# Window attention and a Mish MLP: two chunks at a time by seven half-matrix products, with weight sums streamed from DRAM

## The chip, the core and the metric

The kernel runs on one core of a Trainium2 chip. A core has five engines with an instruction queue each: TensorE (PE) multiplies matrices into PSUM, VectorE (DVE), ScalarE (ACT) and GpSimd (POOL) work on tiles, SyncE (SP) here issues DMAs. The metric is device time in microseconds (us) of one execution; a kernel's time is the median of its runs.

## What is computed

```python
scores = scale * q @ k.T + bias          # 8 batches, 8 heads, 576 tokens, 64 wide; window of 128, causal
attn = exp(scores - max) / (sum + 1e-9)
x = (attn @ v) as [4608 tokens, 512]
h = x @ w_in                              # 512 x 2048
g = h * tanh(log1p(exp(h)))               # Mish
out = g @ w_out                           # 2048 x 512
```

q, k and v are float32, both weights float64 and used with a precision near float32's.

## The kernel before

**Chunks.** The tokens go through the MLP in nine chunks of 512: chunks 0 to 7 are the first 512 tokens of each batch, chunk 8 is the 64 left over from each, which `last_unit` writes to the DRAM tile `xs` and `last_x` reads back. (The change counts them 1 to 9.)

**Split products.** A float32 operand is split into an upper part rounded to TensorE's float32r and a lower part, the rest. A product of two is three matmuls: upper by upper, upper by lower, lower by upper. The upper part is a copy on ACT, the lower one a subtraction on POOL (for attention's output on DVE). Weights are loaded as float64 bits, put together by `convert_w` from shifts on DVE and copies on ACT, split, and stay in SBUF for the whole kernel, sixteen tiles of the tag "w".

**First product** (`first`, line 433): per group of 256 hidden features, 2 x 12 matmuls of 512 tokens, weights stationary, into a double PSUM tile "s"; ACT applies Mish as it reads it, 128x1024 at a time. Eight groups: 192 matmuls.

**Second product** (`parts`, line 452, and `second`, line 484): for half a chunk (256 tokens) and 256 hidden features, `parts` makes gh (ACT) and gl (POOL), 128x512 each, and twelve matmuls use them: the tokens' parts are stationary, 512 columns of w_out move. Sixteen such groups: 192 matmuls. Three buffers each of gh and gl.

**Attention** (`unit` and `last_unit`): per pair of heads two halves; scores (PE), bias and maximum (DVE), exponential (ACT), fold (POOL), scaling (DVE, for the first batch POOL), transposes (PE), masks (DVE), product with v (PE). The attention of chunk c + 1 is put between the matmuls of chunk c's second product.

**Order.** `run` lists of (position, step) are sorted and emitted; PE's and SP's instructions keep that order (`InOrder`, line 20), those of the other engines are placed by the scheduler, with exponentials, Mish and Sign held in order. Loads and stores are issued on SP, in order.

**PSUM.** "s" takes two buffers of two banks, "o" (attention's output), "w" (transposes of `last_unit`), "po0" and "po1" one bank each.

## Time and profile before

| | us |
|---|---|
| runs | 1069.47, 1072.22, 1071.94; median 1071.94 |
| profiled execution, first to last instruction | 1069.5 |
| attention of the first batch, until the first MLP matmul | 88.4 |
| chunk 0 and attention of the second batch | 88.4 to 223.4 |
| a chunk with attention beside it | 111.2 |
| chunks 7 and 8, without attention | 87.0 each |
| DMA traffic | 59.32 MB |

The result lists the times of three runs; for the profiled execution there is the span alone, and it equals the lowest run. The few microseconds outside a span (launch, the last stores) are not in the trace. "Busy" is the time in which an engine's instructions ran; an idle gap is put down to the engine that released the wait. The granted TensorE clock is a share of full speed.

### The profile page before, as it was taken

What the parts mean: (1) busy time and instruction counts of PE and PEld (TensorE: products, weight loads), DVE (VectorE), ACT (ScalarE), POOL (GpSimd) and SP (SyncE); (2) the same over time, 40 slices, a digit from 0 to 9 for tenths busy, and PEclk for the clock granted to TensorE, in tenths of its full rate; (3) what the DMA queues carried; (4) which work ended last, traced back from release to release, by engine and by line L of the source; (5) the groups of instructions that cost most, each with busy time, mean ns of one, the idle gap of its engine ahead of it and who ended that gap; (6) DMA issues with size and microseconds to landing.
All of it is one profiled execution on the core that took longest, in us unless ns stands there. A gap on an engine that the chain in (4) does not pass through costs nothing.

```text
span 1069.5 us, 14242 instructions
## 1 busy us (share of the span) xinstructions
PE 999.0 (93%) x5280; PEld 786.4 (74%) x5280; DVE 418.9 (39%) x1155; ACT 398.6 (37%) x937; POOL 330.8 (31%) x281
## 2 busy tenths in 40 slices
PE   3547985999999999999999999999999999999998
PEld 2336863788778877787778777877788778888886
DVE  4788088710762057304650375027601770000000
ACT  3454455421543245324432353234333442221221
POOL 2464557510441034202421233114310440042032
PEclk9667997999999999999999999999999999999999
DMA  8940011300221002200320021002200201000001
GB/s 277 398 150 4 1 65 36 90 32 1 60 62 62 1 29 88 68 1 25 92 67 1 24 85 56 21 9 72 72 32 1 61 32 42 10 31 20 1 1 40
DMA packets 52133, 59.32 MB, mean 55 GB/s; under 512 B 13024, under 2 KB 32608, under 8 KB 52064
## 3 DMA queue, kind: packets, MB, share of 16 engines
q1 hardware_dynamic: 50880, 57.69, 16.8%
q8 instruction: 42, 0.69, 0.3%
q10 hardware_dynamic: 1184, 0.72, 0.2%
q14 instruction: 27, 0.22, 0.1%
HBM read 47.91 MB, written 10.49 MB: 55 GB/s over the span
## 4 chain that ended last, share of the span: by engine, by line
PE 82%; POOL 1%; ACT 0%; DVE 0%; issue 0%; POOLq 0%
PE po L30 36%; PE h L30 33%; PE s L30 8%; PE o L30 5%; POOL gl L30 0%; POOL so L30 0%; PE pt_3l L30 0%; PE pt_2l L30 0%; PE pt_1l L30 0%; PE pt_0l L30 0%; DVE pz L30 0%; ACT to L30 0%; ACT ob L30 0%; ACT so L30 0%; POOLq L30 0%
## 5 line engine op out<-in xcount | busy, mean ns | idle before, releaser
L30 PE MATMUL h<-x,si 128*128 128x512 f32 x1728 | 394.6, 390 | 0.0
L30 PEld LDWEIGHTS h<-x,si 128*128 128x128 f32 x1728 | 325.2, 188 | 68.0 <-issue 0.3
L30 PE MATMUL po<-so,gh 128*128 128x512 f32 x1152 | 326.5, 405 | 5.0 <-POOL so L30 2.4
L30 POOL TENSOR_TENSOR gl<-g,gh 128x512 fp32r<-128x512 f32 x144 | 195.2, 1356 | 370.6 <-ACT gh L30 346.0
L30 PEld LDWEIGHTS po<-so,gh 128*128 128x128 f32 x1152 | 207.7, 190 | 55.4 <-ACT x L30 6.6
L30 DVE CUSTOM_DVE_ANT_0 pz<-s,nb 128x256 f32<-128x256 f32 (+1 forms) x256 | 84.6, 387 | 339.9 <-PE s L30 339.9
L30 PE MATMUL po<-so,gl 128*128 128x512 f32 x576 | 179.6, 393 | 0.7 <-POOL gl L30 0.7
L30 ACT ACTIVATE g<-h 128x1024 f32<-128x1024 f32 x72 | 74.0, 1028 | 267.7 <-PE h L30 267.7
L30 ACT ACTIVATE pz<-pz,mx 128x256 f32<-128x256 f32 (+1 forms) x256 | 120.3, 471 | 111.8 <-DVE mx L30 111.7
L30 POOL TENSOR_TENSOR pz<-pz 128x256 f32<-128x256 f32 x64 | 65.3, 1020 | 309.6 <-PE po L30 170.0
L30 ACT ACTIVATE gh<-g 128x512 fp32r<-128x512 f32 x144 | 90.6, 629 | 115.2 <-PE po L30 110.8
L30 PEld LDWEIGHTS po<-so,gl 128*128 128x128 f32 x576 | 108.8, 189 | 25.2 <-POOL gl L30 1.1
L30 DVE TENSOR_TENSOR pz<-s,masks 128x1024 f32<-128x1024 f32 x64 | 78.2, 1223 | 28.7 <-PE s L30 28.7
L30 DVE TENSOR_TENSOR pz<-pz,sm 128x512 f32<-128x512 f32 x56 | 59.3, 1058 | 9.4 <-POOL pz L30 7.3
L30 DVE COPY ob<-po 128x512 f32<-128x512 f32 x18 | 12.4, 691 | 124.8 <-PE po L30 124.8
L30 PE MATMUL s<-ident,pz 128*128 128x128 f32 x256 | 41.9, 290 | 19.7 <-DVE pz L30 10.4
L30 PE MATMUL s<-qk 64*128 64x128 f32 (+1 forms) x448 | 57.7, 376 | 0.0
L30 PEld LDWEIGHTS s<-ident,pz 128*128 128x128 f32 x256 | 33.1, 148 | 31.1 <-POOL pz L30 10.5
L30 PE MATMUL o<-pz,va 128*64 128x128 f32 (+1 forms) x560 | 54.9, 325 | 0.0
L30 PEld LDWEIGHTS o<-pz,va 128*64 128x64 f32 x560 | 33.3, 136 | 27.8 <-issue 9.5
L30 ACT ACTIVATE x<-o 128x512 fp32r<-128x512 f32 x32 | 19.1, 598 | 84.1 <-PE o L30 84.1
L30 ACT ACTIVATION_READ_ACCUMULATOR pz<-pz,mx 128x1 f32 x256 | 48.0, 187 | 0.0
(122 smaller groups left out, 577.4 us busy)
## 6 DMA issues: line engine op xcount, KB each, us to landing
wi<-in_moe_w_in_dram SPq DMA_DIRECT2D x16, 512.0 KB, 10.1
wo<-in_moe_w_out_dram SPq DMA_DIRECT2D x16, 512.0 KB, 10.2
out_dram<-ob SPq DMA_DIRECT2D x32, 256.0 KB, 2.0
qk<-in_q_dram SPq DMA_DIRECT2D x28, 288.0 KB, 3.6
qk<-in_k_dram SPq DMA_DIRECT2D x28, 288.0 KB, 3.9
va<-in_v_dram SPq DMA_DIRECT2D x28, 256.0 KB, 2.9
first<-in_q_dram SPq DMA_DIRECT2D x4, 288.0 KB, 4.1
first<-in_k_dram SPq DMA_DIRECT2D x4, 288.0 KB, 4.4
```

What stands on the lines that cost most here:

```text
L30: ins = method(*args, **kwargs)
```

## The change

Chunk 1 is computed as before in plain products, but with weights stationary in both, and output in transposed form. Chunks 2 to 9 go in four pairs. For a pair, the two products are seen as 2x2 blocks: the contraction in halves, the outputs in halves, and the pair's two chunks as the halves of the tokens. Strassen's form in Winograd's variant then takes seven block products instead of eight:

- of the weights, A11, A12, A22 and the sums S1 to S4; of the tokens, B11, B21, B22 and the sums T1 to T4 (`ORDER_I`, `ORDER_O`, `MOVING`);
- first product (`quad`): for each of eight tiles t of the hidden features, seven products of six matmuls with 512 moving columns; p1, s5 and one output are copied by ACT, four sums of PSUM and SBUF are DVE's, one sum of two SBUF tiles is POOL's. Mish (`mish_of`) works afterwards in SBUF on 128x2048, two tiles in a row;
- second product (`right`, `second`): for each of the seven products m and each of eight tiles t, gh and gl of 128x512 and six matmuls; where the block is one of T1 to T4, DVE first adds or subtracts two quarters of the tile g, in place;
- `prepare`: a pair's token blocks come from raw attention output; 8 sums on DVE, 14 splits of 128x512 (ACT and POOL), most of them during the second product of the pair before. For pair 4 the left-over tokens are loaded from `xs` four steps before it begins.

The weights no longer stay in SBUF. `convert_w` also writes each value to DRAM (`vals_i`, `vals_o`, on ACT's DMA queue); `keep_plain` writes the split A11, A12 and A22 there; `combine` reads values back, makes S1 to S4 on POOL, splits them (ACT, POOL on 128x2048) and writes them out: for w_in in the second product of chunk 1, for w_out in the first product of pair 1. `load_stream` brings the split blocks back, 30 loads of 0.75 or 1 MB for each pair, three buffers, each issued when the buffer's last user is past.

PSUM: four single banks for products, "s" one buffer, "t" one bank for the transposes, "o" one. Attention of two batches is spread evenly over chunk 1 (batches 2 and 3) and over pairs 1 and 2; pair 3 carries the last batch, pair 4 none. The output is stored transposed and put in order on the host.

```diff
+ORDER_I = ("A11", "S1", "A12", "S2", "S3", "S4", "A22")
+ORDER_O = ("A11", "S3", "S2", "A22", "S1", "S4", "A12")
+MOVING = {"A11": "B11", "A12": "B21", "A22": "T4", "S1": "T1", "S2": "T2", "S3": "T3", "S4": "B22"}
...
+    def combine(kind, jj, make_hi, make_lo):
...
+        def work():
+            hi, lo = make_hi(f"Sh{kind}{jj}", F32R), make_lo(f"Sl{kind}{jj}", F32R)
+            tt = pool.tensor_tensor
+            tt(out=V[:, 0], in0=V[:, 2], in1=V[:, 0], op=ALU.add)
+            tt(out=V[:, 2], in0=V[:, 1], in1=V[:, 2], op=ALU.subtract)
+            tt(out=V[:, 1], in0=V[:, 0], in1=V[:, 1], op=ALU.subtract)
+            tt(out=V[:, 3], in0=V[:, 3], in1=V[:, 1], op=ALU.subtract)
+            flat = V.rearrange("p b n -> p (b n)")
+            act.activation(hi, flat, AF.Copy)
+            tt(out=lo, in0=flat, in1=hi.bitcast(F32), op=ALU.subtract)
...
+    def split_x(n, blk, pos, src):
...
+        act.activation(x[:, 0, :], src, AF.Copy)
+        pool.tensor_tensor(out=x[:, 1, :], in0=src, in1=x[:, 0, :].bitcast(F32), op=ALU.subtract)
...
+    def halves_of(key, src):
+        gh = small(0, f"gh{key}", F32R)
+        gl = small(1, f"gl{key}", F32R)
         act.activation(gh, src, AF.Copy)
         pool.tensor_tensor(out=gl, in0=src, in1=gh.bitcast(F32), op=ALU.subtract)
+        parts[key] = (gh, gl)
...
+    def quad(n, t, m):
...
+        b = {"A11": 0, "A12": 0, "S1": 1, "S4": 1, "S2": 2, "S3": 3, "A22": 3}[blk]
+        fresh = blk in ("A11", "S1", "S2", "S3")
...
+        for pos in range(2):
+            for w_, x_ in ((0, 0), (0, 1), (1, 0)):
                 k += 1
                 pe.matmul(
+                    o, lhsT=w[:, w_, pos * P : (pos + 1) * P], rhs=x[:, pos, x_, :],
+                    start=(fresh and k == 1), stop=(k == 6), skip_group_check=True,
                 )
...
+            act.activation(qs["p1"], o, AF.Copy)
...
+            dve.tensor_tensor(out=qs["c"], in0=o, in1=qs["s5"], op=ALU.add)
...
+            pool.tensor_tensor(out=g[:, 3, :], in0=qs["c"], in1=qs["u"], op=ALU.add)
+            dve.tensor_tensor(out=g[:, 2, :], in0=o, in1=qs["u"], op=ALU.add)
...
+    def right(n, m, t):
...
+        new = {
+            "T3": (1, 3, 1, ALU.subtract), "T2": (1, 1, 0, ALU.add),
+            "T4": (0, 2, 1, ALU.subtract), "T1": (1, 3, 1, ALU.subtract),
+        }.get(blk)
+        if new:
+            o, a, b, op = new
+            dve.tensor_tensor(out=g[:, o, :], in0=g[:, a, :], in1=g[:, b, :], op=op)
+        at_ = new[0] if new else {"B11": 0, "B12": 1, "B21": 2, "B22": 3}[blk]
+        halves_of(f"{n + 1}_{m}_{t}", g[:, at_, :])
...
+    def second(n, m, t):
...
+            for k, (g, w_) in enumerate(((gh, 0), (gh, 1), (gl, 0))):
+                pe.matmul(
+                    o, lhsT=w[:, w_, d * P : (d + 1) * P], rhs=g,
...
+        for t in range(NT):
+            for m in range(7):
+                steps.append((7 * t + m, lambda t=t, m=m: quad(n, t, m)))
+            steps.append((14 * (t // 2) + 15.2 + 0.01 * (t % 2), lambda t=t: mish_of(n, t)))
+        for m in range(7):
+            for t in range(NT):
+                at_ = 7 * NT + NT * m + t
+                steps.append((at_, lambda m=m, t=t: second(n, m, t)))
+                steps.append((at_ - 2.4, lambda m=m, t=t: right(n, m, t)))
```

More of the change, by code (lines that the diff above doesn't have):

```diff
@@ L196, in load_first @@
         cs = slice(p * P, (p + 1) * P)
-        t = big(f"first{p}", F32)
+        t = (stream if p < 3 else big)(f"first{p}", F32)
         qk = t[:, : 2 * S].rearrange("p (a s) -> p a s", a=2)
@@ L235, in attention_mish_mlp, with raw_x @@
     HEAD = [slice(i * D, (i + 1) * D) for i in range(2)]
+    def raw_x(n, h):
+        if (n, h) not in xr:
+            xr[n, h] = xp.tile([P, 2, 2, CH], F32, tag=f"x{h}", name=f"xr{n}_{h}")
+        return xr[n, h]
     def unit(b, p, half):
@@ new lines, in second_plain @@
+    def second_plain(i):
+        j, a = divmod(i, 2)
+        gh, gl = parts.pop(f"0_{i}")
+        for d in range(4):
+            if i == 0:
+                po[d] = bank(d, f"p0_{d}")
+            for n, (g, w_) in enumerate(((gh, 0), (gh, 1), (gl, 0))):
+                col = 1024 * a + 512 * w_ + P * d
+                pe.matmul(
+                    po[d], lhsT=split[("o", j)][:, col : col + P], rhs=g,
+                    start=(i == 0 and n == 0), stop=(i == NF - 1 and n == 2),
+                )
+            if i == NF - 1:
+                if d == 0:
+                    obs[0] = stage("ob0").rearrange("p (d n) -> p d n", n=CH)
+                ob = obs[0][:, d, :]
+                if d % 2:
+                    act.activation(ob, po[d], AF.Copy)
+                else:
+                    dve.tensor_copy(ob, po[d])
@@ new lines, in store_out @@
+    def store_out(n, d, r, c):
+        load(out[d, :, 2 * n + 1 + c, :], obs[n + 1, d % 2][:, r, :])
+    def second(n, m, t):
+        blk = ORDER_O[m]
+        gh, gl = parts.pop(f"{n + 1}_{m}_{t}")
+        w = wst[n, 2 * NT + 2 * m + t // 4][:, t % 4]
+        upper = blk in ("A11", "S2", "S1", "S4")
+        fresh = blk in ("A11", "S3", "S2", "S1", "A12")
+        for d in range(2):
+            b = 2 * (not upper) + d
+            if t == 0 and fresh:
+                po[b] = bank((0, 2, 1, 3)[b], f"p{n + 1}_{m}_{d}")
+            o = po[b]
+            for k, (g, w_) in enumerate(((gh, 0), (gh, 1), (gl, 0))):
+                pe.matmul(
+                    o, lhsT=w[:, w_, d * P : (d + 1) * P], rhs=g,
+                    start=(fresh and t == 0 and k == 0), stop=(t == NT - 1 and k == 2),
+                    skip_group_check=True,
+                )
+            if t < NT - 1:
+                continue
+            if m == 0:
+                obs[n + 1, d] = stage(f"ob{n + 1}_{d}").rearrange("p (r n) -> p r n", n=CH)
+            p1, u, c, y = (obs[n + 1, d][:, r, :] for r in range(4))
+            add = dve.tensor_tensor
+            if blk == "A11":
+                act.activation(p1, o, AF.Copy)
+            elif blk == "S3":
+                act.activation(c, o, AF.Copy)
+            elif blk == "S2":
+                add(out=u, in0=o, in1=p1, op=ALU.add)
+                pool.tensor_tensor(out=c, in0=c, in1=u, op=ALU.add)
+            elif blk == "A22":
+                add(out=y, in0=o, in1=u, op=ALU.add)
+            elif blk == "S1":
+                add(out=c, in0=o, in1=c, op=ALU.add)
+            elif blk == "S4":
+                add(out=u, in0=o, in1=u, op=ALU.add)
+            elif blk == "A12":
+                add(out=p1, in0=o, in1=p1, op=ALU.add)
@@ L507, in attention_mish_mlp, with run @@
+    DONE = {"A22": (2, 3, 0), "S1": (2, 2, 1), "S4": (0, 1, 1), "A12": (0, 0, 0)}
+    def run(steps):
+        for _, work in sorted(steps, key=lambda s: s[0]):
+            work()
     for p in range(NP):
         load_first(0, p)
-    conv = [(kind, j) for kind in "io" for j in range(NJ)]
-    for w in conv[:-1]:
-        load_w(*w)
+    for j in range(NJ):
+        load_w("i", j)
+    for j in range(3):
+        load_w("o", j)
+    conv = [("i", j) for j in range(NJ)] + [("o", j) for j in range(NJ)]
@@ new lines, in attention_mish_mlp, with spread, of_first @@
+    steps = attention(0) + [(k, lambda: convert_next(2)) for k in (3.6, 5.6, 7.6)]
+    run(steps)
+    def spread(batches, start, space):
+        return [(start + space * (2 * NP * i + s), f) for i, b in enumerate(batches) for s, f in attention(b)]
+    steps = []
+    for i in range(NF):
+        def of_first(i=i):
+            while ("i", i // 2) not in split:
+                convert_next(0)
+            first_plain(i)
+            if i % 2:
+                convert_next(0)
+        steps.append((2 * i, of_first))
+        if i % 2:
+            steps.append((2 * i + 0.2, lambda j=i // 2: keep_plain("i", j)))
+            if 3 + i // 2 < NJ:
+                steps.append((2 * i + 0.3, lambda j=3 + i // 2: load_w("o", j)))
+        if i % 4 == 3:
+            steps.append((2 * i + 2.5, lambda i=i: mish(g0[i // 4].rearrange("p f n -> p (f n)"))))
@@ new lines, in attention_mish_mlp, with of_second @@
+    for i in range(NF):
+        def of_second(i=i):
+            while ("o", i // 2) not in split:
+                convert_next(1)
+            second_plain(i)
+        steps.append((32 + 2 * i, of_second))
+        steps.append((32 + 2 * i - 4.5, lambda i=i: halves_of(f"0_{i}", g0[i // 4][:, i % 4, :])))
+        if i % 2:
+            steps.append((32 + 2 * i + 0.2, lambda j=i // 2: keep_plain("o", j)))
+            steps.append((32 + 2 * i + 0.3, lambda: convert_next(1)))
+    steps.append((65.5, lambda: load(out[:, :, 0, :].rearrange("d p n -> p d n"), obs[0])))
```

389 lines of the change are left out of this document (253 added, 136 removed).

## The prediction

> **What bounds the kernel now.** First the page's busy times and its span in 40 slices: PE = TensorE, DVE = VectorE, ACT = ScalarE, POOL = GpSimd.
>
> ```profile
> PE 999.0 (93%) x5280; PEld 786.4 (74%) x5280; DVE 418.9 (39%) x1155; ACT 398.6 (37%) x937; POOL 330.8 (31%) x281
> PE   3547985999999999999999999999999999999998
> POOL 2464557510441034202421233114310440042032
> ```
>
> PE is full from the ninth slice (about 215 us) to the end; before that it is not. Then the chain of waits in order of time (start, length, what):
>
> ```profile
> 223.43 43.52 PE h L30 x192
> ...
> 334.67 43.52 PE h L30 x192
> ...
> 890.83 43.52 PE h L30 x192
> 934.35 43.52 PE po L30 x192
> ```
>
> 192 matmuls of 512 columns take 43.52 us, 0.2267 us each, in either MLP product. A chunk with attention takes 334.67 - 223.43 = 111.24 us, and 111.24 - 2 x 43.52 = 24.2 us of that is one batch of attention. Third, busy times by stage:
>
> ```profile
> core 0: us, PE busy (x) PEld busy (x) DVE busy (x) ACT busy (x) POOL busy (x), PEclk, DMA share, GB/s
> 0.00:88.40 88.40, 38.63 (x229) 25.99 (x229) 62.73 (x159) 36.92 (x103) 38.61 (x50) 0.73 0.72 251
> 88.40:134.80 46.40, 46.40 (x207) 37.94 (x205) 17.76 (x26) 25.23 (x37) 24.87 (x19) 0.97 0.02 4
> 134.80:223.40 88.60, 72.50 (x411) 53.36 (x411) 67.68 (x159) 43.75 (x116) 48.20 (x37) 0.90 0.19 60
> 267.00:334.70 67.70, 67.70 (x421) 51.78 (x422) 44.19 (x134) 30.61 (x92) 25.79 (x21) 1.00 0.22 65
> ```
>
> From 267 us PE is busy 67.70 of 67.70 us, POOL 25.79. So PE matmuls bound the steady part, and the change removes matmuls. The question is what the other engines must do per matmul that is left.
>
> **What is removed.** A pair of chunks costs 4 x 192 = 768 matmuls now, and 672 after (seven products x 8 tiles x 6, twice). Four pairs: 384 matmuls, 384 x 0.2267 = 87.0 us, all on PE's path. With nothing else late: 1069.5 - 87.0 = 982.5 us.
>
> **What is added in the second product of a pair.** Each of the 56 steps (seven products, eight tiles) is six matmuls, 1.36 us of PE, and needs its own gh (ACT) and gl (POOL), 128x512. Before, one such gh and gl fed twelve matmuls, 2.72 us. In 32 of the 56 steps (T3, T2, T4, T1) DVE first forms a sum of two SBUF tiles. The POOL rows: alone, and back to back.
>
> ```profile
> L30 POOL TENSOR_TENSOR gl<-g,gh 128x512 fp32r<-128x512 f32 x13 | 16.8, 1292 | 44.3 <-ACT gh L30 44.3
> 118.94 2.58 POOL L30 TENSOR_TENSOR si<-wi,si 128x512 fp32r<-128x512 f32 x2 [2.70 <-ACT si L30]
> 121.48 1.32 POOL L30 TENSOR_TENSOR so<-wo,so 128x512 fp32r<-128x512 f32 x1
> ```
>
> Two in 121.48 - 118.94 = 2.54 us: 1.27 us each, just under PE's 1.36. By itself that would fit. But the timeline shows what a DVE operation with two SBUF operands does to POOL:
>
> ```profile
> 284.27 1.23 DVE L30 TENSOR_TENSOR pz<-s,masks 128x1024 f32<-128x1024 f32 x1 [0.37 <-PE s L30]
> 284.30 1.29 POOL L30 TENSOR_TENSOR gl<-g,gh 128x512 fp32r<-128x512 f32 x1 [4.09 <-PE s L30]
> ...
> 301.45 1.29 POOL L30 TENSOR_TENSOR gl<-g,gh 128x512 fp32r<-128x512 f32 x1 [0.42 <-ACT gh L30]
> 301.59 1.69 DVE L30 TENSOR_TENSOR pz<-pz,sm 128x512 f32<-128x512 f32 x1
> ...
> 315.51 0.69 DVE L30 TENSOR_TENSOR pz<-pz,sm 128x512 f32<-128x512 f32 x1
> 315.53 1.82 POOL L30 TENSOR_TENSOR gl<-g,gh 128x512 fp32r<-128x512 f32 x1 [0.42 <-ACT gh L30]
> ```
>
> With one operand in PSUM (s) both run side by side at full speed. With both in SBUF they exclude each other: DVE's 0.69 becomes 1.69, ending 0.54 us after POOL's end; and where DVE came first, POOL's 1.29 becomes 1.82, 0.53 more. So such a DVE operation takes 0.55 us out of POOL's time. A step with a sum costs 1.27 + 0.55 = 1.82 us of what I call the shared time; PE needs 1.36. The small buffers (three gh, three gl) let POOL run ahead by three steps only, so it cannot be evened out over the pair.
>
> The Trainium skill ("SBUF — State Buffer", Who interferes with whom) has this as a rule: the pair of ports is a lock that the first taker holds for the whole instruction, for a DVE instruction with two SBUF inputs against a GpSimd instruction that reads SBUF. By it the hold would be the whole 0.69 us, 0.14 more than the row, or 4 x 32 x 0.14 = 18 us on the sum below; the row decides.
>
> Pair 4 (no attention beside it): four products with sums, 32 x 1.82 = 58.2; three without, PE-bound, 24 x 1.36 = 32.6; two output sums on POOL, 2.5. Together 93.4 us where PE needs 336 x 0.2267 = 76.2: 17.2 over. The other pairs also carry attention (one batch in the second product for pairs 1 and 2, half for pair 3) and the preparation of the next pair:
>
> ```profile
> L30 POOL TENSOR_TENSOR pz<-pz 128x512 f32<-128x512 f32 x32 | 41.3, 1291 | 76.8 <-ACT pz L30 76.8
> L30 POOL TENSOR_TENSOR pz<-pz 128x256 f32<-128x256 f32 x32 | 24.0, 749 | 232.8 <-PE po L30 170.0 <-ACT pz L30 62.9
> ```
>
> Of a batch of attention, folds take (4 x 1.29 + 4 x 0.75) = 8.2 us, scalings 8 x 0.55 = 4.4, small operations some 1.4 (estimate): 14.0. The preparation is 14 low halves x 1.27 = 17.8 and 8 sums x 0.55 = 4.4. Steps alone are 58 x 1.27 + 32 x 0.55 = 91.3. Pairs 1 and 2: 91.3 + 14.0 + 22.2 = 127.5 against PE's 76.2 + 24.2 = 100.4: 27.1 over, each. Pair 3: 91.3 + 7.0 + 5.1 (four low halves; the rest comes at the very end) = 103.4 against 88.3: 15.1 over. Sum: 17.2 + 54.2 + 15.1 = 86.5 us. The second products give back what the matmuls saved: 982.5 + 86.5 = 1069.0.
>
> **The stage until pair 1.** Attention 0 ends as now, at 88.4 us. Then now come chunk 1 and one batch, 135.0 us for 2 x 43.52 + 24.2 = 111.2 of PE path; 23.8 are lost there already. After, a second batch joins (159.2 in the 982.5) and so do the weight sums. Shared time: 26 converted halves, 72 us (1.27 on POOL, two 0.55 and a 0.28 on DVE; five of them 1.27 more for signs); sums of w_in, 4 x (4 x 1.27 + 5.1) = 40.7; factors of pair 1, 22.2; halves of chunk 1, 20.3; two batches, 28.0. In all 183; some 11 fall behind the stage's last matmul, some 10 before 88.4: 162. The 0.28 is from
>
> ```profile
> 142.77 1.27 POOL L30 TENSOR_TENSOR gl<-g,gh 128x512 fp32r<-128x512 f32 x1
> 142.82 1.50 DVE L30 TENSOR_SCALAR wo<-to 128x512 uint32<-128x512 uint32 x1
> ```
>
> (144.32 against 144.04). Full, the stage takes 162 us; filled as now (POOL 24.87 + 48.20 plus about 25 of DVE, 98 of 135, 73%), 222. I take 195, +36 (bounds +3 and +63), since ACT is nearly as full, about 165 us (an estimate) of conversions, copies, Mish, table loads and DMA issues, of which the exponentials of two batches are two eighths of
>
> ```profile
> L30 ACT ACTIVATE pz<-pz,mx 128x256 f32<-128x256 f32 x192 | 95.2, 497 | 36.5 <-DVE mx L30 36.5
> L30 ACT ACTIVATION_READ_ACCUMULATOR pz<-pz,mx 128x1 f32 x256 | 48.0, 187 | 0.0
> ```
>
> and of the shorter ones, some 45 us. The stage's DMA, about 46 MB, goes at this rate:
>
> ```profile
> q1 hardware_dynamic: 50880, 57.69, 16.8%
> ```
>
> 57.69 MB in 16.8% of 1069.5 us is 321 GB/s: 143 us, covered, though little cover is left. The added SP issues (about 120) are near 0.4 us each:
>
> ```profile
> 289.67 0.42 SPq L30 DMA_DIRECT2D qk<-in_k_dram  x1
> ```
>
> **First products.** All four product banks are single. A12 waits for ACT's copy of A11 out of its bank, A22 for DVE's sum out of S3's, with one product (1.36 us) between. A copy or sum from PSUM takes 0.6 to 0.7:
>
> ```profile
> L30 ACT ACTIVATE x<-o 128x512 fp32r<-128x512 f32 x32 | 19.1, 598 | 84.1 <-PE o L30 84.1
> L30 DVE TENSOR_TENSOR x<-o,x 128x512 fp32r<-128x512 f32 x32 | 22.1, 691 | 53.2 <-ACT x L30 53.2
> L30 ACT ACTIVATE g<-h 128x1024 f32<-128x1024 f32 x72 | 74.0, 1028 | 267.7 <-PE h L30 267.7
> L30 ACT ACT_TABLE_LOAD x15 | 19.2, 1283 | 0.3
> ```
>
> It is covered unless ACT is in exponentials or two Mish of 2048 (about 2 us each, and two table loads). I take 0.4 us a tile, a wait of two exponentials with their read-outs (1.3 us above) in one tile of three: 4 x 8 x 0.4 = 13 (bounds 0 and 30). PE has no order to go round such a wait; behind it stand the next products and attention. Shared time there (folds, one POOL sum a tile, in pair 1 also 40.7 for w_out) stays under PE's 100: nothing.
>
> **Head of pair 4.** The leftover tokens are loaded four steps before its start; ten low halves and eight sums, 17.1 us of shared time, must go before T4 is used 8.2 us in: +8 (bounds 0 and 17).
>
> **Streams.** 29.4 MB a pair, with 7 MB for q, k and v 36.4 MB; at 321 GB/s 113 us of about 200: hidden, three buffers ahead. A load waits on SP for its buffer; q, k, v and the stores stand behind it.
>
> **Packing of the second products.** A step's chain is the sum (0.55 after up to 1.27 of POOL), the copy gh, the half gl:
>
> ```profile
> L30 ACT ACTIVATE gh<-g 128x512 fp32r<-128x512 f32 x144 | 90.6, 629 | 115.2 <-PE po L30 110.8 <-ACT g L30 0.4
> ```
>
> 1.82 + 0.63 + 1.27 = 3.7 us against the 4.1 of three PE steps. A mask operation of attention (DVE, 1.23 above) in front of the sum makes it 0.8 late, and behind that gl wait folds and low halves. There are 20 masks in the second products: 16 us if each one empties POOL, nothing if none does. I take 10.
>
> Sum: 1069.0 + 36 + 13 + 8 + 10 = 1136 against the profiled 1069.5. The median of runs, 1071.94, stands 2.4 above that span: 1138.
>
> **Rivals.**
> (a) Forecast, DVE and POOL together bound the second products: 0.74.
> (b) Faster: the sums find time in which POOL stands. It decides at (10.9 - 8 x 1.27) / 8 = 0.09 us: if a sum costs POOL less than that, all second products stay PE-bound, since POOL alone (99.5 in pairs 1 and 2) is under 100.4. Then 982.5 + 36 + 13 + 8 + 2.4 = 1042, and 1006 if the first stage also hides. For it: T3's sums write a free quarter of the tile and can go early. Against: the 1.82 row, and the other 24 sums overwrite what the product before still reads. 0.12.
> (c) Streams do not keep up: below 29.4 MB / 171 us = 172 GB/s they bound pair 4 and soon the others. At 160, pair 4 takes 184 and pair 3 206, some 23 more than the sum, and waits at pieces: 1160 to 1175. Against: 251 GB/s over the first 88.4 us. 0.08.
> (d) The second products eat the saving and all else hides: 1069.0 + 2.4 = 1071, no change. 0.04.
> (e) The matmuls do not go at 0.2267 (other operands streaming, clock): nothing saved, above 1160. The granted clock fell to 0.90 at PE 82% busy, and 76.2 / 0.9 = 84.7 is still below 93.4. 0.02.
>
> **Numbers.** Low end: the bounds at nothing, 1069.0 + 3 + 2.4 = 1075; high: all upper bounds at once, 27 + 17 + 9 + 6 = 59 more, give 1197; I take 1195, which holds (c) too. Below 1075 lie (b) and (d), 0.16. A measurement here can tell 0.3% from no change. Slower 0.74 + 0.08 + 0.02 = 0.84, same 0.04, faster 0.12.
>
> **What would show it.** PE matmuls 3456 to 3072 of 512 columns, 0.227 each. Pair 4's second product near 93 us, not 76; pairs 1 and 2 near 127; in them PE waits for gl of POOL, POOL has hardly an idle gap and gl averages above 1.5 us, DVE's sums above 1.2. First products near PE's time. Pair 1 begins near 283. Second products at 76 and 100 us, or long waits for streamed tiles, would prove me wrong.

## The result and the profile after

| | before | after |
|---|---|---|
| median of the runs, us | 1071.43 (1069.47 to 1072.22, 4 runs) | 1223.13 (1220.54 to 1227.12, 4 runs) |
| ratio | 1 | 1.1425, 95% interval 1.1396 to 1.1453 |
| span of the profiled execution, us | 1069.5 | 1223.5 |
| mean granted TensorE clock | 0.967 | 0.91 |

The change costs 14%. The direction was forecast, the size was not: 1223 lies above the range of 1075 to 1195. The top of the page of after, busy times and 40 slices of the span:

```profile
PE 984.2 (80%) x4896; PEld 736.2 (60%) x4896; DVE 690.1 (56%) x1435; ACT 574.9 (47%) x1187; POOL 678.5 (55%) x513
...
PE   3557887665096989798999997889899889799978
...
POOL 2453446889346618689311187893116689412987
```

PE is busy 14.8 us less than before, not 87, and is hardly ever full; the slice from 306 to 336 us is zero. POOL's digits reach 8 and 9 only in the second products, chunk 1's and the pairs'. The view of busy times by stretch, cut at the first matmul of each product (chunk 1's two, a pause, then the two of pair 1, of pair 3 and of pair 4):

```profile
core 0: us, PE busy (x) PEld busy (x) DVE busy (x) ACT busy (x) POOL busy (x), PEclk, DMA share, GB/s
89.10:184.70 95.60, 77.49 (x435) 57.63 (x433) 64.57 (x181) 60.00 (x140) 35.00 (x28) 0.91 0.62 187
184.70:294.80 110.10, 77.06 (x410) 56.97 (x408) 81.66 (x144) 55.61 (x122) 90.29 (x60) 0.86 0.47 154
294.80:335.00 40.20, 0.00 (x0) 0.02 (x1) 6.15 (x4) 4.96 (x7) 18.16 (x9) 0.53 0.79 259
335.00:469.20 134.20, 112.97 (x587) 83.39 (x588) 75.88 (x191) 68.16 (x142) 64.20 (x42) 0.94 0.73 245
469.20:591.60 122.40, 105.64 (x543) 78.09 (x542) 83.68 (x147) 60.69 (x129) 100.27 (x75) 0.96 0.48 161
833.20:933.80 100.60, 94.36 (x472) 74.18 (x471) 47.95 (x129) 49.58 (x98) 20.08 (x18) 0.97 0.53 174
933.80:1035.60 101.80, 92.08 (x431) 69.91 (x430) 53.47 (x78) 48.91 (x86) 83.34 (x63) 0.97 0.49 168
1035.60:1128.80 93.20, 81.58 (x337) 63.63 (x336) 35.62 (x45) 33.32 (x43) 26.14 (x20) 0.96 0.50 167
1128.80:1219.80 91.00, 84.06 (x337) 63.09 (x335) 40.38 (x35) 37.06 (x58) 79.10 (x57) 0.96 0.45 157
```

Set against PE's path (336 x 0.2267 = 76.2 a product, and 24.2 / 8 = 3.025 for each half of attention; the trace has 10 of a pair's 16 halves in the first product and 6 in the second, where I had 8 and 8; pair 3 has 5 and 3):

| | length (pairs 1 to 4) | PE's path | lost | forecast |
|---|---|---|---|---|
| stage until pair 1 | 95.6 + 110.1 + 40.3 = 246.0 | 159.2 (what the 982.5 holds) | 86.8 | 36 |
| first products | 134.2, 118.0, 100.6, 93.2 | 106.4, 106.4, 91.3, 76.2 | 65.7 | 13 + 8 |
| second products | 122.4, 123.5, 101.8, 90.9 | 94.3, 94.3, 85.3, 76.2 | 88.5 | 86.5 + 10 |

982.5 + 86.8 + 65.7 + 88.5 = 1223.5, the span. So the term that the forecast argued longest about came out right, and the two that it settled by a quick estimate were each some 45 to 50 us short. Where each of the three comes from:

**Second products: the sums and POOL.** The groups of the low halves and of the sums, and the timeline of pair 4's second product, where runs of one operation are one row (the pieces of DVE, then of POOL):

```profile
L30 POOL TENSOR_TENSOR gl<-g,gh 128x512 fp32r<-128x512 f32 x240 | 333.3, 1406 | 59.2 <-ACT gh L30 55.2
...
L30 DVE TENSOR_TENSOR g<-g 128x512 f32<-128x512 f32 x128 | 140.1, 1125 | 40.8 <-ACT g L30 28.4
```

```profile
1141.68 10.17 DVE L30 TENSOR_TENSOR g<-g 128x512 f32<-128x512 f32 x6
```

```profile
1142.76 8.55 POOL L30 TENSOR_TENSOR gl<-g,gh 128x512 fp32r<-128x512 f32 x5
```

Six sums take 10.17 us, 1.70 each, and five low halves 8.55, 1.71: the two alternate, one for one. A step with a sum therefore costs 1.70 us; less the 1.27 of a lone gl, the sum holds POOL up for 0.43, not for the 0.55 that I took. Here the page "SBUF — State Buffer" of the Trainium skill (Who interferes with whom) would have the hold as long as the whole sum, 0.69; the measured 0.43 is below it, and further below than the 0.55 of before's trace.

**First products: the copy behind Mish.** The chain of waits in pair 4's first product (start, length, what):

```profile
1077.08 0.70 DVE g L30
...
1077.88 1.91 ACT g L30
1079.80 0.49 ACT p L30
...
1080.33 3.69 PE q L30 x15
```

DVE's last sum of a tile releases Mish (ACT g, 1.91 us); the copy p1 of A11 stands behind it on ACT, and A12, which needs that bank, starts at 1080.33, 0.04 after the copy. Tiles of pair 4 come 10.40 us apart where seven products take 9.52.

**The stage: weight sums one after the other.** The chain through the pause before pair 1, two groups of sums of w_in and their stores and loads:

```profile
293.31 1.92 ACT Shi L30
295.30 4.51 POOL Sli L30
299.83 0.36 SPq L30
...
306.33 4.12 DMA Vi<-vals_i
310.59 1.27 POOL Vi L30
...
314.61 1.26 POOL Vi L30
315.90 1.92 ACT Shi L30
317.89 4.50 POOL Sli L30
322.41 0.36 SPq L30
```

From Sli to Sli is 317.89 - 295.30 = 22.6 us, with nothing of one group beside the next: split, lower half, eight stores issued by SP, then the loads of the next group, then four sums. The first streamed tile of pair 1 is ready 40.3 us after the last matmul of chunk 1. In pair 1 the same stores, of w_out, stand on SP in front of a streamed tile; SP waits for POOL's Slo, then issues eight, and only then the load for which PE waits:

```profile
379.27 4.62 POOL Slo L30
...
383.91 0.36 SPq L30
...
388.82 7.36 DMA ws<-wq_i
...
396.23 2.93 PE q L30 x6
```

**Matmuls at half speed.** That last row holds what I had not looked for: six matmuls in 2.93 us, where six at 0.2267 are 1.36. Busy times around it, by stretch (the clock is the sixth figure):

```profile
388.40:396.30 7.90, 0.07 (x1) 0.07 (x1) 0.69 (x1) 0.00 (x0) 3.74 (x3) 0.79 0.94 311
396.30:401.00 4.70, 4.70 (x28) 3.28 (x30) 0.91 (x2) 1.91 (x1) 2.29 (x3) 0.62 1.02 380
401.00:410.00 9.00, 6.97 (x36) 5.27 (x32) 7.08 (x22) 7.59 (x14) 5.57 (x3) 1.00 0.81 269
```

While PE stood, and for some 3.6 us after, the granted clock was below full (0.50 from 393.1 to 399.8 us in narrower windows, 1.00 behind that). Over the whole trace of after 151 of the 512-column matmuls, in bursts of up to 12 at a granted clock of 0.50, follow each other at 0.427 us instead of 0.2267: 151 x 0.20, about 30 us lost, spread over all three terms above. In the trace of before it is 14 matmuls, 3 us. Of after's pauses of PE (start to start, less 0.25 us) such a burst followed 14 of 19 that were longer than 3 us, 7 of 15 between 2 and 3, and 3 of 24 between 1 and 2. The Trainium skill ("TensorE: Matmul & The Clock Gate", Part 1) says that the clock falls to half after an idle window of some 3.4 us that runs freely, until PE has been busy for one; the trace agrees on the half speed (0.50) and on the length (its stretches at 0.50 last 3.4 us or a multiple of that), but here shorter pauses did it too.

**Transposes of the left-over tokens.** The groups of PE's transposes, with the idle time in front of them, first those of before, then those of after:

```profile
L30 PE MATMUL pt_1l<-ident,pz_1l 128*128 128x128 f32 x8 | 2.3, 290 | 0.0
```

```profile
L30 PE MATMUL pt<-ident,pz 128*128 128x128 f32 x256 | 42.8, 294 | 39.0 <-DVE pz L30 22.4 <-POOL pz L30 11.9 <-DVE xo_0l L30 3.8
...
L30 PE MATMUL pt_1l<-ident,pz_1l 128*128 128x128 f32 x8 | 2.9, 362 | 16.8 <-DVE pz L30 14.6 <-ACT pz L30 2.2
```

The four groups pt_0l to pt_3l have 0.0 before and 6.8 + 16.8 + 11.8 + 11.9 = 47.3 after, in 32 transposes. In the timeline of pair 1's second product, the masks on DVE and those transposes on PE:

```profile
499.56 1.21 DVE L30 TENSOR_TENSOR pz<-pt,masks 128x1024 f32<-128x1024 f32 x1
...
527.51 1.21 DVE L30 TENSOR_TENSOR pz<-pt,masks 128x1024 f32<-128x1024 f32 x1
```

```profile
500.83 0.48 PE L30 MATMUL pt_1l<-ident,pz_1l 128*128 128x128 f32 x1 [5.56 <-DVE pz L30]
...
528.77 0.33 PE L30 MATMUL pt_2l<-ident,pz_2l 128*128 128x128 f32 x1 [2.91 <-DVE pz L30]
```

499.56 + 1.21 = 500.77 and 527.51 + 1.21 = 528.72: each starts 0.05 to 0.06 us after a mask has been applied to the halves' transposes. Before, those went into a buffer of "s" and the left-over tokens' into "w"; the change gives both the one bank "t", so PE stands until DVE, which is behind with its work, has emptied it. Of the 47.3 us, waits that DVE's pz ended make 33.4; the rest ended on other steps of attention.

### The profile page after: what moved, and what is told of

It reads as the page before. It is cut to its first block, busy times and chain, and to the rows that moved or that the text cites. A ratio compares the mean times of both kernels' runs of the same rounds, so it can differ in the third digit from the quotient of the medians.

```text
span 1223.5 us, 15061 instructions
## 1 busy us (share of the span) xinstructions
PE 984.2 (80%) x4896; PEld 736.2 (60%) x4896; DVE 690.1 (56%) x1435; ACT 574.9 (47%) x1187; POOL 678.5 (55%) x513
## 4 chain that ended last, share of the span: by engine, by line
PE 39%; DVE 15%; POOL 14%; ACT 11%; DMA 9%; issue 9%; SPq 3%; ACTq 0%; POOLq 0%; DVEq 0%
PE p L30 16%; PE q L30 13%; DVE g L30 5%; POOL gl L30 4%; DVE pz L30 4%; ACT g L30 4%; ACT pz L30 3%; PE s L30 3%; SPq L30 3%; PE o L30 3%; PE h L30 2%; POOL x_T L30 2%; ACT L30 2%; DMA wi<-in_moe_w_in_dram 2%; DMA Vo<-vals_o 2%
## 5 line engine op out<-in xcount | busy, mean ns | idle before, releaser
L30 POOL TENSOR_TENSOR gl<-g,gh 128x512 fp32r<-128x512 f32 x240 | 333.3, 1406 | 59.2 <-ACT gh L30 55.2
L30 PE MATMUL p<-gh,ws 128*128 128x512 f32 x896 | 292.8, 409 | 6.6 <-ACT gh L30 6.1
L30 PE MATMUL q<-x_T,ws 128*128 128x512 f32 x768 | 203.8, 406 | 18.4 <-DMA ws<-wq_i 9.3
L30 PE MATMUL q<-x_B,ws 128*128 128x512 f32 x576 | 157.7, 411 | 67.1 <-DMA ws<-wq_i 41.6
L30 PE MATMUL p<-gl,ws 128*128 128x512 f32 x448 | 184.9, 413 | 21.0 <-POOL gl L30 20.1
L30 PEld LDWEIGHTS p<-gh,ws 128*128 128x128 f32 x896 | 170.3, 195 | 45.1 <-ACT gh L30 7.5
L30 ACT ACTIVATE pz<-pz,mx 128x256 f32<-128x256 f32 (+1 forms) x256 | 120.3, 471 | 134.2 <-DVE mx L30 128.8
L30 PEld LDWEIGHTS q<-x_T,ws 128*128 128x128 f32 x768 | 146.1, 195 | 56.1 <-DMA ws<-wq_i 10.2
L30 PEld LDWEIGHTS q<-x_B,ws 128*128 128x128 f32 x576 | 109.2, 195 | 96.9 <-issue 42.4
L30 DVE TENSOR_TENSOR g<-g 128x512 f32<-128x512 f32 x128 | 140.1, 1125 | 40.8 <-ACT g L30 28.4
L30 PEld LDWEIGHTS p<-gl,ws 128*128 128x128 f32 x448 | 87.1, 194 | 58.8 <-POOL gl L30 40.9
L30 POOL TENSOR_TENSOR g<-c,u 128x512 f32<-128x512 f32 x32 | 41.6, 1300 | 131.6 <-DVE c L30 114.6
L30 PE MATMUL o<-pz,va 128*64 128x128 f32 (+1 forms) x560 | 58.5, 342 | 12.5 <-DVE pz L30 12.5
```

The lines of the kernel that those rows point to most:

```text
L30: ins = method(*args, **kwargs)
```

## The experiments

Two causes were set against each other first: **exclusion** (DVE's sums and POOL's halves share their time; what PE waits for is arithmetic) and **order** (PE and SP keep their fixed order, and wait for a step that stands late in another engine's queue; less arithmetic would change little). All edits are to the kernel after; times in us. The kernel before ran beside each and took 1069.9 to 1070.9. Versions 1 to 16 were run once each, and differences of a few us between them mean nothing. Lengths of all stages (first / second product; chunk 1's second with the pause behind it):

| run | time | chunk 1 | pair 1 | pair 2 | pair 3 | pair 4 |
|---|---|---|---|---|---|---|
| after | 1223.1 | 95.6 / 150.4 | 134.2 / 122.4 | 118.0 / 123.5 | 100.6 / 101.8 | 93.2 / 90.9 |
| 1 no sums | 1173.9 | 96.8 / 150.0 | 132.2 / 109.8 | 115.0 / 109.9 | 100.7 / 89.8 | 95.9 / 78.4 |
| 2 gl on DVE | 1181.9 | 95.5 / 150.3 | 132.1 / 113.7 | 115.0 / 113.7 | 100.5 / 92.6 | 95.7 / 79.0 |
| 3 early sums | 1191.5 | 101.7 / 114.8 | 132.0 / 122.6 | 116.5 / 122.6 | 101.3 / 102.0 | 93.3 / 91.0 |
| 4 p1 on DVE | 1204.9 | 96.5 / 150.6 | 135.2 / 123.6 | 112.2 / 122.6 | 91.0 / 101.8 | 85.9 / 91.2 |
| 5 late stores | 1221.7 | 94.4 / 151.5 | 130.6 / 122.5 | 116.5 / 122.6 | 99.6 / 101.8 | 96.0 / 90.7 |
| 6 no weight sums | 1176.9 | 96.4 / 110.6 | 127.5 / 122.6 | 116.3 / 123.6 | 100.6 / 101.8 | 93.1 / 90.9 |
| 7 gl mixed | 1180.7 | 94.5 / 151.0 | 134.3 / 112.4 | 116.5 / 112.5 | 99.6 / 92.7 | 93.8 / 79.1 |
| 8 all repairs | 1124.1 | 101.1 / 116.0 | 120.8 / 114.0 | 106.6 / 114.6 | 91.0 / 110.2 | 76.2 / 79.2 |
| 9 transposes late | 1137.4 | 104.2 / 112.2 | 120.0 / 123.5 | 107.9 / 120.7 | 91.0 / 108.5 | 76.2 / 79.5 |
| 10 more buffers | 1090.6 | 90.9 / 107.7 | 116.6 / 113.4 | 106.6 / 114.3 | 91.0 / 100.4 | 76.2 / 76.7 |
| 11 as 8, no weight sums | 1087.4 | 94.9 / 98.2 | 111.5 / 112.3 | 106.6 / 114.0 | 91.0 / 109.4 | 76.2 / 79.5 |
| 12 attention first | 1114.8 | 89.9 / 110.6 | 134.3 / 108.4 | 119.4 / 108.8 | 104.5 / 90.7 | 76.2 / 76.7 |
| 13 scaling on ACT | 1087.0 | 88.1 / 106.4 | 118.5 / 114.6 | 106.7 / 114.9 | 91.0 / 99.1 | 76.2 / 76.7 |
| 14 both | 1087.7 | 89.4 / 105.3 | 125.0 / 103.3 | 118.2 / 103.3 | 103.6 / 90.9 | 76.2 / 76.6 |
| 15 all gl on DVE | 1088.4 | 87.7 / 106.4 | 124.8 / 105.6 | 118.1 / 105.1 | 103.6 / 88.8 | 76.2 / 77.0 |
| 16 most gl on DVE | 1083.6 | 87.8 / 106.0 | 124.6 / 105.1 | 116.6 / 103.1 | 103.7 / 88.0 | 76.2 / 77.0 |
| 17 as 13, most gl on DVE | 1082.3 | 85.3 / 106.3 | 118.9 / 112.5 | 106.7 / 114.7 | 91.0 / 97.9 | 76.2 / 77.0 |
| 18 later attention | 1097.7 | 92.1 / 124.6 | 118.0 / 110.4 | 107.1 / 108.3 | 92.2 / 101.3 | 76.2 / 76.6 |

### 1 and 2: second products, the sums and the low halves

```diff
-        if new:
-            o, a, b, op = new
-            dve.tensor_tensor(out=g[:, o, :], in0=g[:, a, :], in1=g[:, b, :], op=op)
```

> Leaves out the 32 sums a pair (T1 to T4 of the hidden features) that DVE makes ahead of the second product; the quarter of g that they would have overwritten is used as it is. Theory (a sum of two SBUF tiles on DVE and an operation of POOL exclude each other): pair 4's second product falls from 91.0 us to 78, PE's 76.2 and a little; pairs 1 and 2 from 122.4 and 123.6 to about 108 (24 to 32 holds of 0.43 to 0.55 gone), total about 1223 - 50 = 1173. Rival (the chain ACT copy, POOL half, three buffers is what PE waits for, or the streamed weights are late): the second products stay within 3 us of 91, 122 and 124 and the total within 10 us of 1223. First products and the stage before pair 1 do not change by either.

```diff
-        pool.tensor_tensor(out=gl, in0=src, in1=gh.bitcast(F32), op=ALU.subtract)
+        eng = pool if key[0] == "0" else dve
+        eng.tensor_tensor(out=gl, in0=src, in1=gh.bitcast(F32), op=ALU.subtract)
```

> In the second products of the four pairs the lower half gl is subtracted by DVE instead of POOL; nothing is left out. Theory (exclusion, so the shared time counts, and DVE takes 0.6 us where POOL takes 1.27): pair 4's second product is PE-bound, 91 to 77; in pairs 1 and 2 DVE becomes the fullest engine (56 x 0.6 + 32 x 0.6 + attention's 28 + 13 = 94 us beside PE's 94), so 122 to between 98 and 112; total about 1223 - 14 - 2 x 18 - 10 = 1165. Rival (PE waits for the length of the chain, not for POOL's time): gl gets only 0.6 us shorter, second products 91 to 88 and 122 to 118; total above 1205. Rival 2 (DVE too full): pairs 1 and 2 get slower than 122.

Busy times of pair 1's and pair 4's second products in run 1, and the group of gl on DVE in run 2:

```profile
468.70:578.50 109.80, 101.24 (x543) 75.32 (x542) 57.95 (x121) 60.96 (x129) 96.79 (x75) 1.00 0.53 178
...
1089.80:1168.20 78.40, 77.27 (x337) 62.48 (x335) 6.69 (x10) 37.19 (x58) 72.50 (x57) 1.00 0.52 182
```

```profile
L30 DVE TENSOR_TENSOR gl<-g,gh 128x512 fp32r<-128x512 f32 x224 | 170.7, 771 | 53.6 <-ACT gh L30 46.9 <-PE p L30 4.0 <-POOL g L30 2.5
```

Without the sums pair 4 takes 78.4 against 90.9, with POOL at 72.50 of 78.40 and the clock at 1.00: exclusion. With the sums kept and gl on DVE at 0.77 us it takes 79.0, though every step has the same chain, so it was not the chain. But pairs 1 and 2 stay 15 us above PE's path even with no sum, at the full clock. Of the 88.5 us lost in second products exclusion therefore makes up at most 12.6 + 13.6 + 12.0 + 12.5 = 50.7 (after against run 1, which also takes the sums' own time off DVE); the other 38 or more are something else, and my sum came out right partly by luck.

### 3 and 6: the stage

```diff
-        steps.append((34 + 7 * jj, begin))
-        steps.append((35 + 7 * jj, middle))
-        steps.append((39.5 + 7 * jj, lambda jj=jj: stores[jj, 1]()))
+        steps.append((12.5 + 8 * jj, begin))
+        steps.append((14.5 + 8 * jj, middle))
+        steps.append((19.5 + 8 * jj, lambda jj=jj: stores[jj, 1]()))
```

> The weight sums of w_in are started 20 positions earlier, in the first product of chunk 1, where POOL was busy 35 of 95.6 us. Theory (the 40.3 us in which PE waits for pair 1's first streamed block are the end of a chain: values loaded, four sums, two splits, stores on SP, then the next group, each some 22 us, begun too late): the wait falls from 40 to under 8 us, chunk 1's second product gets shorter by up to 15 since 40 us of POOL's work leave it, its first product longer by up to 15; total 1175 to 1190. Rival (the stage's shared time or its DMA is the bound wherever the sums lie): pair 1 begins within 10 us of 335 and the total stays above 1213.

```diff
-            tt(out=V[:, 0], in0=V[:, 2], in1=V[:, 0], op=ALU.add)
...
-            tt(out=lo, in0=flat, in1=hi.bitcast(F32), op=ALU.subtract)
+            act.activation(lo[:, :8], flat[:, :8], AF.Copy)
+            lo = hi
```

> Leaves out the arithmetic of the weight sums on POOL, both kinds: the values are loaded, ACT rounds them, and that one tile is stored as both halves; all DMAs stay. Theory (the late start of pair 1 is the chain loads, sums, splits, stores, one group after the other, and not DMA): a group takes 12 us instead of 22, the wait before pair 1 falls from 40 to 5 to 20 us; pair 1's first product falls from 134 to about 124, since SP no longer stands before late stores; total 1180 to 1200. Chunk 1's second product (110 us) stays within 4 us, since there PE waits in its fixed order for transposes whose operands DVE makes late. Rival (POOL's 40 us of sums are what fills that stage): the second product falls to 100 or less. Rival 2 (DMA): nothing changes by more than 5 us.

With the sums of w_in twenty positions earlier the pause goes from 40.3 to 5.1 us, and the span with it. That the second product would become shorter as well was wrong: 114.8 - 5.1 = 109.7, as before; but POOL is still busy 84.14 us there (90.29 of 110.1 in after), as a part of the sums still falls into it. Without POOL's arithmetic it is 110.6 - 17.4 = 93.2, against the expectation that it would stay, and a pause of 17.4 is left. So both were true, each of another part: the pause is order, and the product's length hangs on POOL's sums. PE itself waits there for transposes that DVE's pz holds up (20.0 us in after, 2.7 in run 6), so the sums seem to reach it by way of DVE; that is argued, not shown.

### 4 and 5: first products

```diff
-            act.activation(qs["p1"], o, AF.Copy)
+            dve.tensor_copy(qs["p1"], o)
```

> In the first products of the pairs the copy of A11's result out of its bank is DVE's instead of ACT's. Theory (PE waits at A12 for that copy because a Mish of 1.91 us, or two, stand ahead of it on ACT): a tile of pair 4 falls from 10.40 to 9.5 us, its first product from 93.2 to 87 (the start's 10 us stay); pairs 2 and 3 gain 2 to 6 us each; total 1200 to 1212. Rival (the bank's turn-round is too long by itself: the copy waits for A11's end and PE for the copy, whoever makes it): tiles stay at 10.3 to 10.5, total within 5 us of 1223.

```diff
-                steps.append((3.5 + 8 * jj, middle))
-                steps.append((9.4 + 8 * jj, lambda jj=jj: stores[jj, 3]()))
+                steps.append((5.5 + 8 * jj, middle))
+                steps.append((13.4 + 8 * jj, lambda jj=jj: stores[jj, 3]()))
```

> In pair 1's first product the sums of w_out are made two positions later and their stores stand four positions later on SP; nothing else moves. Theory (SP works in order and stands before stores whose lower halves POOL has not made, so loads of streamed blocks behind them come too late; 11 us of waiting for streams): the waits of PE for streamed blocks in pair 1 fall from 10.6 to under 4 us and its first product from 134.2 to 122 to 128; total 1211 to 1217. Rival (the streams are late because DMA is full there, 245 GB/s with the sums' traffic): the product stays at 131 to 136.

The chain of run 4 in pair 4's first product, where after has the wait for ACT in every tile:

```profile
1069.78 22.44 PE q L30 x99
```

Ninety-nine matmuls, 0.2267 us each, without a break: the copy behind Mish was the wait. Pair 3 falls from 100.6 to 91.0 (its path is 91.3), pair 4 to 85.9, with its head left over. The stores explain only 3.6 us of pair 1's excess; most of that expectation missed.

### 7 and 8: the repairs together

```diff
-        halves_of(f"{n + 1}_{m}_{t}", g[:, at_, :])
+        halves_of(f"{n + 1}_{m}_{t}", g[:, at_, :], dve if new else pool)
```

> In the second products DVE subtracts gl in the 32 steps for which it also makes the sum, POOL in the other 24. Nothing is left out. Theory (shared time: 0.55 + 0.5 in steps with a sum, 1.27 in the others, both under PE's 1.36; DVE 20 us less full than with all gl on it): second products 78 in pair 4, 87 to 91 in pair 3, 102 to 112 in pairs 1 and 2 (79.0, 92.6 and 113.7 with all on DVE); total 1165 to 1180. Rival (the change of engine between products costs order, or DVE is the limit again): pairs 1 and 2 at 114 or more.

With nothing left out, run 7 takes 10.0 + 11.0 + 9.1 + 11.8 = 41.9 us off the second products. Pair 4 comes to 79.1; pairs 1 and 2, at 112.4 and 112.5, stay just outside what was expected.

Run 8 is this with runs 3, 4 and 5, the copy s5 on DVE too, and the left-over tokens of pair 4 loaded 18 positions before pair 3's end instead of 4, with pair 4's factors spread over those:

> Everything at once: sums of w_in early, their stores and those of w_out's sums later, copies of A11 and S1 on DVE, gl split between DVE and POOL, and pair 4's left-over tokens loaded 18 positions before its start with its factors prepared from there. Theory (the losses are separate and add: 32 + 8 + 25 + 45 + 8): 1223 - 118 = 1105, range 1095 to 1120; still above the kernel before, because chunk 1's stage keeps some 55 us over PE's path. Rival (they hide one another, DVE being the next limit): above 1135.

The gains nearly add up: 99 us less than after, where 118 were expected, so the run misses its range by 4. Pair 4's first product is 76.2, its path to the tenth, so its head (the tokens loaded late) is gone; pair 3 pays for it in its second product, 110.2 against 92.7 in run 7.

### 9, 10 and 11: what is left

```diff
-            (1.3, weights), (1.99, values), (2.02, evict),
+            (1.55, weights), (1.99, values), (2.02, evict),
```

> On top of everything at once (1124.1): attention's transposes stand 0.25 of a unit later in TensorE's fixed order; nothing is left out. Theory (what is left in chunk 1's stage, 58 us over PE's path, and in pairs 1 to 3's second products, 20 to 25 each, is DVE and POOL being full, so that PE's order makes it wait sooner or later): the total stays within 8 us of 1124. Rival (DVE has time enough and is only late for the place that TensorE's order gives the transposes): the 50 us of waits for transposes fall by half, total 1095 to 1110.

```diff
-        return ff.tile([P, 512], dtype, tag=("gh", "gl")[which], name=name, bufs=3)
+        return ff.tile([P, 512], dtype, tag=("gh", "gl")[which], name=name, bufs=5)
...
-                steps.append((at_ - 2.4, lambda m=m, t=t: right(n, m, t)))
+                steps.append((at_ - 4.4, lambda m=m, t=t: right(n, m, t)))
```

> On top of everything at once (1124.1): five buffers of gh and gl instead of three and halves made 4.4 steps ahead instead of 2.4 (one buffer of 8 KB a partition given up for it). Nothing is left out. Rival (second products lose to bursts: an attention operation in front of a sum, with only three steps in reserve): pairs 1 to 3's second products fall from 114, 115 and 110 to below 105, total about 1095. Theory (DVE's and POOL's shared time): they fall by 0 to 4 us each, total 1112 to 1126.

Run 11 is run 8 with the edit of run 6:

> On top of everything at once (1124.1), leaves out the arithmetic of the weight sums on POOL, both kinds; the DMAs and ACT's rounding stay. Theory (POOL's and DVE's shared time fills chunk 1's stage, 40 us of it the sums): the stage, 217 us, falls by 20 to 35, pair 1's first product from 121 to 110 to 116; total 1085 to 1102. Rival (with the sums started early, the stage is bound by DVE's conversions and attention alone, POOL's sums lie beside them): the stage stays within 8 us of 217, total above 1112.

Moving the transposes alone made it worse by 13 us. The values stayed in place, and PE's waits there, o behind DVE's pz, grew from 22.5 to 27.0 us, while those of the halves' transposes fell from 42.2 to 35.5: in part the wait only changed hands. The buffers brought 34 us, but elsewhere than expected: in the stage (217.1 to 198.6) and in pairs 3 and 4, while the second products of pairs 1 and 2 stayed at 114. So it is not the depth of the buffers that holds those two, and why the stage gained isn't shown. Run 11 takes nothing out of them (112.3 and 114.0), since the weight sums lie elsewhere; it confirms what they cost there: the stage falls from 217.1 to 193.1, pair 1's first product from 120.8 to 111.5, both as expected.

### 12 to 18: the second products of pairs 1 and 2

Run 12 is run 10 with the attention packed towards the first product, and with pair 4's left-over tokens and factors made earlier; 13 is run 10 with the scaling of the weights on ACT; 14 has both; 15 and 16 are run 14 with gl on DVE in all steps, and in those with a sum and all odd tiles.

```diff
-            space = (END - 8.0) / (halves + 2.02)
+            space = 4.4 if len(batches) == 2 else 5.3
```

> On top of the deeper buffers (1090.6): the attention beside pairs 1 and 2 is spread over their first 80 positions of 112 instead of all, so that 12 or 13 of 16 halves lie in the first product; beside pair 3 all eight; its left-over tokens are loaded and pair 4's factors made earlier. Nothing is left out. Theory (second products are over PE's path since DVE's and POOL's shared time is full there and has room in the first products, POOL 24 of 107 us): pairs 1 and 2 lose 20 us each in the second product now; of that 10 to 14 go, the first products grow by PE's own path alone (3 us a half, which leaves the second); pair 3 from 191.4 to 184; total 1060 to 1072. Rival (what is lost belongs to attention's chain itself, wherever it lies): first products grow by what second ones lose, total 1086 or more.

```diff
+            for c in range(4):
+                act.activation(st["pz"][:, c, :P], st["pz"][:, c, :P], AF.Copy, scale=st["sm"][:, c : c + 1])
```

> On top of the deeper buffers (1090.6): the scaling of attention's weights goes from DVE (two SBUF operands, 128x512) to ACT in four pieces of 128x128, for batches 2 to 8. Nothing is left out. Theory (shared time): 0.55 us of shared time a half and DVE's wait of 0.5 to 1 go, 56 halves; second products of pairs 1 and 2 gain 3 to 8 us each, chunk 1's stage 3 to 10; total 1065 to 1082. Rival (ACT, with 1.6 us more a half, becomes late for the exponentials and copies): total 1090 or more.

> The two together on top of the deeper buffers. Theory: the gains of both less a third, since both empty the same second products: 1046 to 1062, under the kernel before. Rival (ACT late in the first products, which then hold most exponentials): above 1070.

> On top of both (1087.7): all lower halves of the second products on DVE, so that POOL has only the preparation's halves and folds there. Nothing is left out. Theory (what holds pairs 1 and 2's second products, 103 us against 85 of PE's path with three halves of attention, is the next pair's preparation on the shared time, 14 halves and 8 sums, 22 us, beside 24 x 1.27 + 32 x 1.05 = 64): shared time falls to some 80, DVE is at about 80; the products fall from 103 to 88 to 96, pair 3's from 91 to 80 to 88; total 1055 to 1075. Rival (the preparation's own chain, loads and copies, holds them, or DVE now does): 101 or more, total above 1083.

> As before, with the lower halves of the 24 steps without a sum taken in turn by DVE and POOL (44 on DVE, 12 on POOL). Nothing is left out. Theory: between 1087.7 and the kernel with all on DVE if shared time decides (second products of pairs 1 and 2 at 93 to 100); below it if DVE decides.

What packing takes from the second products it gives to the first ones: 113.4 + 116.6 = 230.0 in run 10, 108.4 + 134.3 = 242.7 in run 12. Runs 13 and 14 stayed outside their ranges, with pairs 1 and 2 unmoved in run 13. Taking all gl from POOL changes nothing any more. In run 15 the chain of pair 2's second product, and the busy times of the same stretch, show what is there instead:

```profile
673.67 1.15 DVE pz L30
...
674.86 0.48 PE pt_3l L30
675.33 5.12 PE p L30 x12
```

```profile
675.30:680.50 5.20, 5.20 (x15) 3.58 (x15) 5.20 (x10) 2.06 (x5) 1.32 (x1) 0.50 0.27 76
```

A mask on DVE, the transpose of left-over tokens 0.04 us behind it, then twelve matmuls in 5.12 us at a granted clock of 0.50. The last two runs (three rounds each) were to tell this from shared time. Run 17 is run 13 with the gl of run 16:

> The version with the scaling on ACT, all other repairs and the even spread of attention (1087.0; second products of pairs 1 and 2 114.6 and 114.9), with gl on DVE also in the odd tiles of the steps without a sum, as in the best version so far. Theory (shared time of DVE and POOL still holds the second products of pairs 1 and 2): they fall to 106 to 109, total 1070 to 1078. Rival (transposes that TensorE meets before DVE and ACT have their operands hold them): they stay within 2 us of 114, total 1083 to 1090.

Run 18 moves transposes, values and evictions of all units later, those of left-over tokens by about as much, and adds a buffer of pz. With five buffers of gh and gl it needs more SBUF than there is (28.25 KB a partition for attention's tiles, with 25.34 left), so it has four of them and a lead of 3.4 positions instead of 4.4:

```diff
-            (1.3, weights), (1.99, values), (2.02, evict),
+            (1.7, weights), (2.5, values), (2.53, evict),
...
-            (0.01, scores), (0.3, exps), (0.9, fold), (1.5, weights), (1.995, values),
+            (0.01, scores), (0.3, exps), (0.9, fold), (1.95, weights), (2.45, values),
```

> The version before (1082.3; P1 and P2 near their lengths with the scaling on ACT), with the transposes 0.4 unit later, values and evictions (unlike in the first trial) 0.5 unit later, and a third buffer of pz so that nothing has to come free earlier; to make room, four buffers of gh and gl instead of five and a lead of 3.4 positions. Theory of the held transposes: the idle time of TensorE in front of transposes, 27 us in the version with the scaling on ACT, falls under 10, and with it go some of the half-speed matmuls; first products of pairs 1 and 2 fall to 108 to 114 and 106, second ones to 100 to 106, total 1045 to 1065. Rival (shared time, or a late DVE in any case: what moves later is late there too): within 5 us of the version before, or slower.

Run 17 took 1082.32 (1.0111 of before, 1.0094 to 1.0128), the lowest of all; run 18 took 1097.74 (1.0238, 1.0205 to 1.0271). The groups of transposes in run 17, then in run 18:

```profile
L30 PE MATMUL pt<-ident,pz 128*128 128x128 f32 x256 | 43.7, 293 | 24.8 <-ACT pz L30 11.9 <-POOL pz L30 7.5 <-DVE xo_2l L30 2.6
L30 PE MATMUL pt_1l<-ident,pz_1l 128*128 128x128 f32 x8 | 3.1, 384 | 23.8 <-DVE pz L30 23.8
```

```profile
L30 PE MATMUL pt<-ident,pz 128*128 128x128 f32 x256 | 43.5, 295 | 21.7 <-DVE xo_0l L30 7.7 <-ACT pz L30 6.9 <-POOL pz L30 2.3
...
L30 PE MATMUL pt_1l<-ident,pz_1l 128*128 128x128 f32 x8 | 2.9, 358 | 15.4 <-DVE pz L30 15.4
```

In run 17 the second products of pairs 1 and 2 stayed at 112.5 and 114.7, with POOL busy 41.07 and 42.37 us of them: not POOL's time. DVE's busy time went from 85.27 us in pair 1's (run 10) to 91.31, and the length didn't follow that either. In run 18 the idle time in front of the halves' transposes fell only from 24.8 to 21.7, that in front of the left-over tokens' stayed (52.5 and 51.6 over the four groups); both sorts moved together and the bank is still one, which may be why. The two products became 2 and 6 us shorter, and the stage 25 us longer (216.7 against 191.6), with one buffer less of gh and gl and the shorter lead: as a repair it failed, and since these changed too it doesn't settle the theory. That the wait for the bank "t" stands in front of these transposes is shown by the rows; what a bank for each would bring wasn't tried.

## Why the prediction was right and wrong

- **What is removed**: right. 4 x 672 = 2688 matmuls of 512 columns in the pairs, 0.2267 us each where PE runs through (run 4's 22.44 for 99).
- **Second products**: 88.5 lost, 96.5 forecast with the packing. The mechanism is shown (runs 1, 2, 7), but as 41.9 (run 7) to 50.7 (run 1) of the 88.5. The hold was 0.43 instead of 0.55, the split 10 to 6 instead of 8 to 8. For the other 38 or more I had 10 of packing and attention's shared time, and what they are stays open: without the sums pairs 1 and 2 lose 15 us each at the full clock, with POOL busy 96.79 of 109.80 in pair 1; in run 17, with POOL at 41.07 of 112.40, they lose 18 and 20, and there PE stands 9 to 10 us in front of transposes and the granted clock is 0.95 and 0.94. That the total came near is luck in this part. gl averaged 1.41 and the sums 1.13, both under what I said would show. Rival (b)'s early sums of T3 did not come: in pair 4 one sum runs ahead, and from 1139.88 us on T3's sums alternate with gl like the others.
- **The stage until pair 1**: this step failed, 86.8 instead of 36. "Full, the stage takes 162 us; filled as now, 222" treated the weight sums as work to be filled in. They are four groups in a row, 22.6 us from one to the next at the end, placed late in the stage, and pair 1 can't start before the last; that is the pause of 40.3, of which run 3 took away 35. Pair 1 began at 335.0, not near 283. With the order alone mended (run 3) the stage takes 216.5, still 21 more than the 195 that I took; with the deeper buffers as well (runs 10, 13, 17) it takes 191.6 to 198.6. So the order of the sums was not looked at, and neither was what three buffers of gh and gl mean for this stage; the amount of work may have been sized rightly. (Its 26 converted halves are 75 us by their own terms, not 72; that changes little.)
- **First products**: failed too, 65.7 instead of 13 + 8. I named the right wait, A12 for ACT's copy, and priced it as one tile in three behind two exponentials. It is each tile of a pair behind Mish of 1.91 us, 0.88 a tile in pair 4. Run 4 takes the wait away in pair 4, and run 8 brings pairs 2, 3 and 4 to PE's path. Pair 1 has besides the weight sums for w_out and stores that stand on SP in front of a load (7.9 us in one place); 10 to 14 us of it are left in the versions that keep the even spread of attention, and 5 in run 11, which has no weight sums.
- **Head of pair 4**: some 10 us (17.0 lost less 8 x 0.88), where I had 8; run 8 removes it.
- **Streams**, rival (c): false as a rate. Waits for streamed tiles are the pause before pair 1 and the load behind the stores, both set by order.
- **Left out**: that a pause costs more than its length. I gave the clock as a loss only while another engine is the bound anyway ("below 93.4"), and left the half-speed bursts, about 30 us of the 154.0 by which the span grew, out of the sum (no run took them away by themselves); nor did I look at which tiles share the new single bank "t".

The two short terms are 50.8 and 44.7, the second products 8.0 the other way: 1136 + 87.5 = 1223.5. The upper end was made of bounds on shared time and on rates; no bound stood for order.

What the change could give at best stays open. The best version is still 1.1% above before. Its losses over the 982.5 (1079.5 - 982.5 = 97) are 32.4 in the stage, 12.5 in pair 1's first product, 18.2, 20.4 and 12.6 in the second products of pairs 1 to 3, and about 1 elsewhere: these eat the 87.0 saved, and a little more.
